# Routing's tiles, the order of loads, and two engine assignments in an attention and mixture-of-experts kernel

## The chip, the cores and the metric

The kernel runs on one core of one Trainium2 chip. The metric is the time on the device of one launch, in microseconds (us); lower is better. Before the change three runs gave 750.35, 750.99 and 751.72 us, a median of 750.99 us.

## What is computed

Three layers run one after the other. The first is bucketed attention over 8 heads of 768 tokens. The second is an expert layer with a top-1 choice and a capacity, the third an expert layer in which all eight experts see all tokens:

```python
x = attention(q, k, v, proj)                       # 768 x 512
logits = x @ w_gate                                # 768 x 8
expert_idx = argmax(logits, axis=1)
gate_w = softmax(logits)[expert_idx]
disp[e, pos] = x[i]                                # token i in the next free slot of its expert e
h = maximum(einsum('ecd,edf->ecf', disp, w1), 0)
y = einsum('ecf,efd->ecd', h, w2)
out[i] = gate_w[i] * y[expert_idx[i], pos[i]]      # the layer's output
P = sinkhorn(exp(out @ w_gate2))                   # 8 rounds of row and column scaling
out2 = sum over e of P[:, e] * (maximum(out @ w12[e], 0) @ w22[e])
```

## The kernel before

TensorE, ScalarE, VectorE and SyncE (DMA issue) execute their instructions in the order in which the program emits them. So the order of the Python calls is the order of each engine's queue.

**Attention** (to about 122 us) runs in an order from a list scheduler. Its tiles lie in pools at the left of on-chip memory and are given back when the function `attention` ends. At the right lie the first raw tiles of weights (`rawx`) behind a block `padx` of 112 words.

**The first expert layer** is `ffn` (L1286). Each expert has a tile of 128 slots. The weights come in 36 pieces of 1 MB (128 x 4 x 512 floats), in the fixed order of `stream`; nine raw tiles hold pieces on their way. `conv_next` (L351) takes the next piece and splits it in two halves: `split_w` (L330) emits for each half a copy by ScalarE that rounds to the high part (L337) and a subtraction that gives the low part (L339). The subtraction is VectorE's, but GpSimd's for both halves of the third piece (i == 2) and for a few later halves (`LO_POOL`). Then `conv_next` issues the load of the piece nine places on (L314, L316, or in four parts at L328). That load waits until the raw tile that it fills has been split.

`dispatch` (L1029) is routing. It is a generator: up to its first `yield`, some 25 short VectorE instructions (L1040 to L1088) find each token's slot, with two small matmuls (L1056, L1057) among 56 + 32 matmuls that only keep TensorE busy (L1055, L1059). Then six indirect DMAs from GpSimd's queue (L1092) scatter the tokens' rows to DRAM, to `xd`. The later parts are taken between the steps of the expert layer. Its small tiles come from a pool `tp` that is opened after attention's pools have been given back, in their place.

After routing, `ffn` issues three loads of slots' rows on SyncE's queue (`load_x`, L1173, from `xd`), splits four pieces (each with its load of a later piece on the same queue), and starts. For the low parts of the fourth piece the calls are kept in `los` and emitted inside the first `stage_a`. That `stage_a` does not read `xd`: it selects expert 0's tokens by a matmul with a one-hot matrix (L1194), copies the high part by ScalarE (L1180) and subtracts the low part by VectorE (L1181), in two halves. For the other experts `stage_a` transposes the loaded rows (L1187).

Then come the 36 steps, one piece of weights each: `g1` (L1201, product L1208, ReLU L1214), `tr` (L1216, transposes L1223, high part L1224, low part L1225) and `g2` (L1227, product L1234). A product takes 12 matmuls of 512 columns; for each of 4 blocks it uses high x high, high x low and low x high, so its second matmul already needs the low part of the weights, and its third the low part of the left factor. Acts such as a transposition are put in the middle of a step. At the end of an expert's second half of `g2`, its result is copied from PSUM to `ysb`, by VectorE (L1252) for experts 0 to 5 and by ScalarE (L1250) for expert 6. A DMA on ScalarE's queue writes it to `yd` (L1254), for experts 0 to 5 one step later. The PSUM tile of the result is one of two that `stage_a` uses as well.

**The second expert layer** (from about 262 us) keeps TensorE busy to 744 us.

Of the kernel before, what the change touches and what calls it, by code (L numbers as in the profile page):

```python
# [8 lines left out]
F32 = mybir.dt.float32  # L9
# [5 lines left out]
AF = mybir.ActivationFunctionType  # L15
# [6 lines left out]
P = 128  # L22
# [6 lines left out]
E = 8  # L29
# [18 lines left out]
POOL_END = 4 * 8 - 2 - NRAW - NRAWX  # L48
HI_DVE = ()
LO_POOL = (1,)  # L50
# [9 lines left out]
SQ = (33, 33)  # L60
CPAD = 0
SPAD = 160
OVR = 64
OVS = S - P
ZROW = E * P + NOV * OVR
# [158 lines left out]
def kernel(ctx: ExitStack, tc: tile.TileContext, consts, q, k, v, proj, wg, w1, w2, wg2, w12, w22, out, cap, dbg=None):  # L224
    nc = tc.nc
    f32 = lambda ap: ap.bitcast(F32)
    V = nc.vector
# [4 lines left out]
    cpool = ctx.enter_context(tc.tile_pool(name="cpool", bufs=1))  # L232
    rawp = ctx.enter_context(tc.tile_pool(name="rawp", bufs=NRAW))
    rawx = ExitStack()
    rawx.enter_context(tc.tile_pool(name="padx", bufs=1, side="right")).tile([P, 112], F32, name="padx")
    rawxp = rawx.enter_context(tc.tile_pool(name="rawx", bufs=NRAWX, side="right"))
    dpool = ctx.enter_context(tc.tile_pool(name="dpool", bufs=1, space=DRAM))

# [18 lines left out]
    seq = list(range(E - 1)) + [E, E - 1]  # L257
# [3 lines left out]
    for i in range(1, NV - 1):  # L261
        e, f = seq[i], seq[i + 1]
# [67 lines left out]
    def split_w(ts, raw, i, late=None):  # L330
        for z, t in enumerate(ts):
            sl = slice(2 * z, 2 * z + 2)
            n = (2 * i + z) % 8
            if 4 <= i < POOL_END and n in HI_DVE:
                V.tensor_copy(t[:, 0], raw[:, sl, :])
            else:
                nc.scalar.activation(out=t[:, 0], in_=raw[:, sl, :], func=AF.Copy)  # L337
            eng = nc.gpsimd if i == 2 or 4 < i < POOL_END and n in LO_POOL else V
            lo = lambda eng=eng, sl=sl, t=t: eng.tensor_tensor(  # L339
                out=t[:, 1], in0=raw[:, sl, :], in1=f32(t)[:, 0], op=ALU.subtract  # L340
            )
            if late is None:
                lo()
            else:
                late.append(lo)
# [5 lines left out]
    def conv_next(eng=nc.sync, late=None):  # L351
        i = cnt["conv"]
        if i >= len(stream) or i >= cnt["used"] + NHL:
            return False
        cnt["conv"] += 1
        raw = raw_t[i] if i == 4 * NV else raw_t.pop(i)
        ts = [hl_tile(2 * i + z) for z in range(2)]
        split_w(ts, raw, i, late)
        hl_t[i] = ts
        if cnt["load"] < cnt["limit"]:  # L360
            load_next(eng)
        return True
# [598 lines left out]
    def open_pool(st, name, bufs, **kw):  # L961
        return st.enter_context(tc.tile_pool(name=name, bufs=bufs, reuse_waits="tile", **kw))
# [63 lines left out]
        V.tensor_scalar(out=s, in0=inv, scalar1=-0.5, scalar2=200.0 * 2 ** 23, op0=ALU.mult, op1=ALU.add)  # L1026
        V.tensor_scalar(out=inv, in0=inv, scalar1=0.5, scalar2=54.0 * 2 ** 23, op0=ALU.mult, op1=ALU.add)

    def dispatch(tp, first, last):  # L1029
        t3 = lambda nm, dt=F32: tp.tile([P, NT, E], dt, name=nm)  # L1030
        te = lambda nm, dt=F32: tp.tile([P, E, NT], dt, name=nm)
        six = tp.tile([P, 8, NT], F32, name="six")
# [8 lines left out]
        cand = t3("cand")  # L1041
# [9 lines left out]
        ps = mm_tile()  # L1051
# [6 lines left out]
        for _ in range(NW[1]):  # L1058
# [3 lines left out]
            out=inc.rearrange("p e t -> p (e t)"), data0=col(C_MASK, E * NT), data1=oh.rearrange("p e t -> p (e t)"),  # L1062
# [16 lines left out]
            out=first, in0=col(C_S, P).unsqueeze(1).to_broadcast([P, NT, P]),  # L1079
# [11 lines left out]
        for t in range(NT):  # L1091
            i = nc.gpsimd.indirect_dma_start(  # L1092
                out=xd, out_offset=bass.IndirectOffsetOnAxis(ap=idxs[:, t:t + 1].bitcast(U32), axis=0),
                in_=x[:, t, :], in_offset=None,
# [8 lines left out]
        V.scalar_tensor_tensor(out=db, in0=jsc, scalar=float(OVR), in1=col(C_CE, E), op0=ALU.mult, op1=ALU.add)  # L1103
        V.tensor_single_scalar(out=keep, in_=pos1, scalar=float(cap), op=ALU.is_le)
        V.tensor_tensor(out=od, in0=oh, in1=xt(db), op=ALU.mult)
        ex = t3("ex")
        V.tensor_tensor(out=ex, in0=lg, in1=bt(mx), op=ALU.subtract)
        V.tensor_reduce(out=dbs, in_=od.rearrange("p e t -> p t e"), axis=AX.X, op=ALU.add)
        V.tensor_scalar_add(dbs, dbs, -float(OVR))
# [46 lines left out]
    def ffn_tools(st, bufs, xbufs):  # L1156
        p2 = open_pool(st, f"f{bufs}", bufs)
        dT, hs, hT, xe, yt = {}, {}, {}, {}, {}
        puts = []

        def onehot():
            t = p2.tile([P, 2, 512], F32, tag="hs", name="hs")
            return t.rearrange("p a n -> p (a n)")[:, 0:NT * P].rearrange("p (t n) -> p t n", n=P)
        W3 = ((0, 0), (0, 1), (1, 0))

        def load_x(e):
            t = p2.tile([P, DM], F32, tag="xe", name="xe", bufs=xbufs)
            r0 = e * P if e < E else E * P + (e - E) * OVS
            if e == E:
                for r in (0, OVR):  # L1170
                    nc.sync.dma_start(out=t[r:r + OVR], in_=xd[r0:r0 + OVR])
            else:
                nc.sync.dma_start(out=t, in_=xd[r0:r0 + P])  # L1173
            xe[e] = t

        def stage_a(e, oh0=None, late=None):
            d = dT[e] = p2.tile([P, 2, 512], F32R, tag="dT", name="dT")

            def split(sl, ps):
                nc.scalar.activation(out=d[:, 0, sl], in_=ps, func=AF.Copy)  # L1180
                V.tensor_tensor(out=d[:, 1, sl], in0=ps, in1=f32(d)[:, 0, sl], op=ALU.subtract)  # L1181

            if oh0 is None:
                t = xe.pop(e)
                ps = y_tile() if e <= E else mm_tile()
                for c in range(4):
                    nc.tensor.transpose(ps[:, c * P:(c + 1) * P], t[:, c * P:(c + 1) * P], ident)  # L1187
                split(slice(0, 512), ps)
                return
            for j in range(2):  # L1190
                ps = y_tile()
                for c in range(2):
                    for t in range(NT):
                        nc.tensor.matmul(  # L1194
                            ps[:, c * P:(c + 1) * P], lhsT=x[:, t, (2 * j + c) * P:(2 * j + c + 1) * P],
                            rhs=oh0[:, t, :], start=(t == 0), stop=(t == NT - 1),
                        )
                split(slice(j * 256, j * 256 + 256), ps[:, 0:256])
                late.pop(0)()

        def g1(e, half, w, mid=None):  # L1201
            if half == 0:
                hs[e] = p2.tile([P, 2, 512], F32, tag="hs", name="hs")
            ps = mm_tile()
            n = 0
            for c in range(4):
                for a, b in W3:
                    nc.tensor.matmul(  # L1208
                        ps, lhsT=dT[e][:, a, c * P:(c + 1) * P], rhs=w(b, c), start=(n == 0), stop=(n == 11)
                    )  # L1210
                    n += 1
                if mid and c == 1:
                    mid()
            nc.scalar.activation(out=hs[e][:, half, :], in_=ps, func=AF.Relu)  # L1214

        def tr(e, half):  # L1216
            if half == 0:
                hT[e] = p2.tile([P, 2, 2, 512], F32R, tag="hT", name="hT")
            h = hs[e] if half == 0 else hs.pop(e)
            ps = mm_tile()  # L1220
            for f in range(4):
                sl = slice(f * P, (f + 1) * P)
                nc.tensor.transpose(ps[:, sl], h[:, half, sl], ident)  # L1223
            nc.scalar.activation(out=hT[e][:, 0, half, :], in_=ps, func=AF.Copy)  # L1224
            V.tensor_tensor(out=hT[e][:, 1, half, :], in0=ps, in1=f32(hT[e])[:, 0, half, :], op=ALU.subtract)  # L1225

        def g2(e, half, w, mid=None):  # L1227
            if half == 0:
                yt[e] = psl.tile([P, 512], F32, tag="l", name="yl") if e >= E else y_tile()
            ps, t = yt[e], hT[e]  # L1230
            n = 12 * half
            for f in range(4):
                for a, b in W3:
                    nc.tensor.matmul(  # L1234
                        ps, lhsT=t[:, a, half, f * P:(f + 1) * P], rhs=w(b, f), start=(n == 0), stop=(n == 23)
                    )
                    n += 1
                if mid and f == 1:
                    mid()
            if half == 0:  # L1240
                return
            hT.pop(e)
            ps = yt.pop(e)
            if e == E:
                return ps
            if e == E - 1:
                return ps
            y = p2.tile([P, DM], F32, tag="ysb", name="ysb", bufs=1)
            if e == E - 2:
                nc.scalar.activation(out=y, in_=ps, func=AF.Copy)  # L1250
            else:
                V.tensor_copy(y, ps)  # L1252
            n, r0 = (P, e * P) if e < E else (OVR, E * P + (e - E) * OVR)
            put = lambda: nc.scalar.dma_start(out=yd[r0:r0 + n], in_=y[0:n])  # L1254
            if e < E - 2:
                puts.append(put)
            else:
                put()

        return onehot, puts, load_x, stage_a, g1, tr, g2  # L1260
# [25 lines left out]
    def ffn():  # L1286
        with ExitStack() as st:
            onehot, puts, load_x, stage_a, g1, tr, g2 = ffn_tools(st, 2, NXE)
            oh0 = onehot()
            ohs = {}  # L1290
            parts = dispatch(open_pool(st, "tp", 1), oh0, onehot)
            next(parts)
            for i in range(1, 4):
                load_x(seq[i])
            los = []
            for i in range(4):
                conv_next(late=los if i == 3 else None)
            done = 0

            def act(s):  # L1300
# [579 lines left out]
```

## Time and profile before

| | us |
|---|---|
| median of three runs | 750.99 |
| the profiled execution, its own time | 749.77 |
| its span, from first to last instruction | 748.0 |
| TensorE (PE) busy | 728.4 (97%) |
| VectorE (DVE) busy | 563.0 (75%) |
| ScalarE (ACT) busy | 467.5 (63%) |
| GpSimd (POOL) busy | 113.0 (15%) |

The granted clock is 1.000 for the whole span. A row of a timeline gives the start and the duration in us, the engine, the line of the kernel, the operation, what it writes and reads, and how many instructions are merged in it. In square brackets stands how long the engine was idle before, and what ended that. PE is TensorE's matmuls, SPq and ACTq the DMA issues of SyncE and ScalarE. Neighbouring matmuls overlap in a row, so the distance from start to start tells their pace.

### The profile page before, as it was taken

To read this page: it belongs to the slowest core of one execution; us is meant where nothing else is said; L and a number is where in the kernel's file an instruction comes from. 1 tells how busy PE (TensorE), PEld (TensorE's weight loads), DVE (VectorE), ACT (ScalarE), POOL (GpSimd) and SP (SyncE) were. 2 spreads that over 40 slices of the span, in tenths; PEclk is the share of its full clock that TensorE was granted. 3 is DMA by queue.
4 is the path that set the end of the run, shared out by engine and by line. 5 is a ranking of instruction groups with operands and counts; after the bars stand their busy time and mean duration, and the time that the engine had idled before them with its cause. 6 is when DMAs were issued, how large, how long until landed. Compare 5 with 4: busy or idle time off the path is not lost.

```text
span 748.0 us, 12294 instructions
## 1 busy us (share of the span) xinstructions
PE 728.4 (97%) x4770; PEld 467.4 (62%) x4770; DVE 563.0 (75%) x983; ACT 467.5 (63%) x761; POOL 113.0 (15%) x117
## 2 busy tenths in 40 slices
PE   8999998999999799999999999999999999999998
PEld 7889888777788556545546545545545545645654
DVE  5988997689998866887695785786785865866842
ACT  4799898488787678555653754664575375365420
POOL 5577863512100200000000000000000000000000
PEclk9999999999999999999999999999999999999999
DMA  9456549799997333422231131041032030000002
GB/s 238 104 142 180 152 142 383 266 376 376 385 389 292 87 113 113 169 77 94 61 110 55 49 121 57 4 164 59 1 114 112 1 113 1 1 0 1 1 1 84
DMA packets 61608, 97.02 MB, mean 130 GB/s; under 512 B 17603, under 2 KB 19059, under 8 KB 61546
## 3 DMA queue, kind: packets, MB, share of 16 engines
q1 hardware_dynamic: 53066, 82.21, 33.2%
q10 hardware_dynamic: 7520, 10.83, 4.1%
q0 software_dynamic: 960, 3.15, 1.3%
q8 instruction: 39, 0.64, 0.4%
q14 instruction: 23, 0.19, 0.1%
HBM read 79.99 MB, written 9.31 MB: 119 GB/s over the span
## 4 chain that ended last, share of the span: by engine, by line
PE 62%; DVE 2%; ACT 1%; issue 0%; DVEq 0%
PE b L1783 32%; PE b L1708 25%; PE b L1751 4%; DVE hl L1429 1%; DVE s L1616 1%; PE b L1546 1%; ACT junk L1009 0%; DVE q L1280 0%; DVE x L1799 0%; PE b L1505 0%; PE b L1017 0%; PE b L1493 0%; ACT hl L1426 0%; PE b L1593 0%; DVE x L1284 0%
## 5 line engine op out<-in xcount | busy, mean ns | idle before, releaser
L1783 PE MATMUL b<-hl,hT 128*128 128x512 f16 (+1 forms) x1176 | 252.0, 375 | 0.0
L1783 PEld LDWEIGHTS <-hT 128*128 128x128 f16 x1176 | 114.3, 98 | 129.1
L1708 PE MATMUL b<-xo,hl 128*128 128x384 f16 x1176 | 192.7, 326 | 0.0
L1708 PEld LDWEIGHTS <-hl 128*128 128x128 f16 x1176 | 114.8, 98 | 77.0 <-issue 0.8
L1429 DVE SCALAR_TENSOR_TENSOR hl<-raw,scl,hl 128x1024 f16<-128x1024 f32 x57 | 72.3, 1281 | 45.2 <-ACT hl L1426 45.2
L339 DVE TENSOR_TENSOR hl<-raw,hl 128x1024 fp32r<-128x1024 f32 x66 | 82.0, 1289 | 4.4 <-ACT hl L337 4.2
L1426 ACT ACTIVATE hl<-raw,scl 128x1024 f16<-128x1024 f32 x57 | 63.3, 1139 | 24.7 <-DVE scl L1020 24.7
L337 ACT ACTIVATE hl<-raw 128x1024 fp32r<-128x1024 f32 x72 | 71.8, 1062 | 0.4 <-ACT ysb L1250 0.4
L1009 ACT ACTIVATE junk<-raw 128x1024 bf16<-128x1024 f32 x64 | 67.2, 1050 | 1.0
L1801 DVE SCALAR_TENSOR_TENSOR x<-b,q,x 128x512 f32<-128x512 f32 (+1 forms) x43 | 31.5, 738 | 34.3 <-PE b L1783 34.0
L1208 PE MATMUL mm<-hl,dT 128*128 128x512 f32 x216 | 54.3, 398 | 1.6 <-DVE dT L1181 1.6
L763 POOL TENSOR_TENSOR plo<-pf,phi 128x768 f16<-128x768 f32 x30 | 49.7, 1666 | 24.6 <-ACT phi L759 12.2
L1681 DVE SCALAR_TENSOR_TENSOR hT<-tz,hT 128x384 f16<-128x384 f32 x44 | 24.1, 556 | 37.6 <-ACT hT L1680 37.5
L1680 ACT ACTIVATE hT<-tc 128x384 f16<-128x384 f32 x28 | 14.7, 525 | 60.1 <-DVE tc L1677 60.1
L1234 PE MATMUL y<-hl,hT 128*128 128x512 f32 x192 | 50.0, 402 | 2.2 <-POOL hl L339 1.1
L698 DVE TENSOR_REDUCE mz<-mm 128x1 f32<-128x384 f32 x96 | 47.6, 550 | 2.9 <-PE mm L691 2.6
L1426 ACT ACTIVATE hl<-s,scl 128x1024 f16<-128x1024 f32 x28 | 31.5, 1148 | 28.4 <-DVE s L1616 21.5
L752 ACT ACTIVATE pf<-mm 128x384 f32<-128x384 f32 x96 | 41.8, 488 | 8.4 <-PE mm L745 6.6
L1208 PEld LDWEIGHTS mm<-hl,dT 128*128 128x128 f32 x216 | 39.4, 188 | 10.6 <-DVE dT L1181 2.4
L745 PE MATMUL mm<-q,k 128*128 128x384 f32 x192 | 45.1, 353 | 0.0
L1234 PEld LDWEIGHTS y<-hl,hT 128*128 128x128 f32 x192 | 34.6, 188 | 11.2 <-POOL hl L339 1.9
L759 ACT ACTIVATE phi<-pf 128x768 f16<-128x768 f32 x46 | 38.7, 848 | 1.2
(280 smaller groups left out, 1003.9 us busy)
## 6 DMA issues: line engine op xcount, KB each, us to landing
raw<-in_moe_w_dram SPq DMA_DIRECT2D x48, 1024.0 KB, 8.3
raw<-in_moe_w_dram SPq DMA_DIRECT2D x48, 256.0 KB, 5.5
raw<-in_moe_w_dram ACTq DMA_DIRECT2D x8, 1024.0 KB, 5.0
xd<-zer SPq DMA_DIRECT2D x13, 256.0 KB, 3.1
xe<-xd SPq DMA_DIRECT2D x7, 256.0 KB
yd<-ysb ACTq DMA_DIRECT2D x7, 256.0 KB, 4.5
qkin<-in_q_dram SPq DMA_DIRECT2D x8, 192.0 KB, 4.6
vin<-in_v_dram SPq DMA_DIRECT2D x4, 384.0 KB
```

The costliest lines, as they stand in the source:

```text
L337: nc.scalar.activation(out=t[:, 0], in_=raw[:, sl, :], func=AF.Copy)
L339: lo = lambda eng=eng, sl=sl, t=t: eng.tensor_tensor(out=t[:, 1], in0=raw[:, sl, :], in1=f32(t)[:, 0], op=ALU.subtract)
L698: V.tensor_reduce(out=mz[h][:, a, t:t + 1], in_=b.ps[:, 0:HW], axis=AX.X, op=ALU.max)
L745: nc.tensor.matmul(ps[:, 0:HW], lhsT=kk[h][:, tok(t)], rhs=qq[h][:, half(a)], start=(i == 0), stop=(i == 1))
L763: eng.tensor_tensor(out=lo[h, t], in0=pf[h, t], in1=hi[h, t], op=ALU.subtract)
L1009: nc.scalar.activation(out=junk[:, 0:n], in_=src, func=AF.Square, accum_out=acc)
L1208: nc.tensor.matmul(ps, lhsT=dT[e][:, a, c * P:(c + 1) * P], rhs=w(b, c), start=(n == 0), stop=(n == 11))
L1234: nc.tensor.matmul(ps, lhsT=t[:, a, half, f * P:(f + 1) * P], rhs=w(b, f), start=(n == 0), stop=(n == 23))
L1426: nc.scalar.activation(out=slot[n][:, 0], in_=src() if src else total[n], func=AF.Copy, scale=sw)
L1429: V.scalar_tensor_tensor(out=slot[n][:, 1], in0=src() if src else total.pop(n), scalar=sw, in1=slot[n][:, 0], op0=ALU.mult, op1=ALU.subtract,)
L1708: nc.tensor.matmul(ps, lhsT=w[:, a, c, j * P:(j + 1) * P], rhs=xo[:, o, b, c, :], start=(n == 0 and not again), stop=(n == 5), skip_group_ ...
L1783: nc.tensor.matmul(ps, lhsT=hT[:, a, 2 * r + f, t * P:(t + 1) * P], rhs=w[:, b, f, cs], start=(r == 0 and n == 0), stop=(r == 3 and n == 5),)
```

## The change

Four edits. Routing's pool `tp` is opened at the start, at the right of memory, in a place of its own; `padx` shrinks from 112 to 40 words, and the tile `ex` uses `cand`'s place. The loads of slots' rows come after the first two calls of `conv_next` (one) and after all four (two), and no longer before them. The third piece's low parts go to VectorE. The results of experts 0 to 5 are copied from PSUM by ScalarE.

```diff
@@ tile_attn_moe_kernel @@
-    rawx.enter_context(tc.tile_pool(name="padx", bufs=1, side="right")).tile([P, 112], F32, name="padx")
+    rawx.enter_context(tc.tile_pool(name="padx", bufs=1, side="right")).tile([P, PADX], F32, name="padx")
+    tp = rawx.enter_context(tc.tile_pool(name="tp", bufs=1, side="right"))
@@ split_w @@
-            eng = nc.gpsimd if i == 2 or 4 < i < POOL_END and n in LO_POOL else V
+            eng = nc.gpsimd if 4 < i < POOL_END and n in LO_POOL else V
@@ dispatch @@
-    def dispatch(tp, first, last):
+    def dispatch(first, last):
...
-        ex = t3("ex")
+        ex = cand
@@ ffn_tools, g2 @@
             y = p2.tile([P, DM], F32, tag="ysb", name="ysb", bufs=1)
-            if e == E - 2:
-                nc.scalar.activation(out=y, in_=ps, func=AF.Copy)
-            else:
-                V.tensor_copy(y, ps)
+            nc.scalar.activation(out=y, in_=ps, func=AF.Copy)
@@ ffn @@
-            parts = dispatch(open_pool(st, "tp", 1), oh0, onehot)
+            parts = dispatch(oh0, onehot)
             next(parts)
-            for i in range(1, 4):
-                load_x(seq[i])
             los = []
             for i in range(4):
                 conv_next(late=los if i == 3 else None)
+                if i == 1:
+                    load_x(seq[1])
+            for i in range(2, 4):
+                load_x(seq[i])
```

## Rows read from the trace of the kernel before

**Rows 1.** TensorE's waits, 120 to 260 us: total, times, longest.
```profile
PE mm L1208 <- DVE dT L1181: 1.6, 2, 1.0
PE y L1234 <- DVE ysb L1252: 1.0, 2, 0.8
```

**Rows 2.** Timeline of DVE, end of attention to the first product.
```profile
122.10 0.21 DVE L793 TENSOR_TENSOR lg<-lg,lt 128x48 f32<-128x48 f32 x1
124.54 0.20 DVE L1040 TENSOR_REDUCE six<-lg 128x6 f32<-128x48 f32 x1 [2.23 <-POOL sv L986]
...
126.23 0.17 DVE L1068 TENSOR_SCALAR ov<-mm 128x8 f32<-128x8 f32 x1
...
128.85 0.17 DVE L1088 TENSOR_TENSOR idxs<-six 128x6 int32<-128x6 f32 x1
128.96 4.63 DVE L339 TENSOR_TENSOR hl<-raw,hl 128x1024 fp32r<-128x1024 f32 x4
133.50 0.42 DVE L1181 TENSOR_TENSOR dT<-y,dT 128x256 fp32r<-128x256 f32 x1
...
134.97 0.42 DVE L1181 TENSOR_TENSOR dT<-y,dT 128x256 fp32r<-128x256 f32 x1
```

**Rows 3.** Timeline of POOL, the same stretch and on.
```profile
123.50 1.01 POOL L814 TENSOR_TENSOR x<-num,eu 128x384 f32<-128x384 f32 x1 [1.49 <-ACT num L809]
...
129.89 1.38 POOL L1092 DMA_INDIRECT xd<-x,idxs  x1 [5.33 <-issue]
...
137.66 0.96 POOL L1092 DMA_INDIRECT xd<-x,idxs  x1 [0.30 <-issue]
138.65 4.72 POOL L339 TENSOR_TENSOR hl<-raw,hl 128x1024 fp32r<-128x1024 f32 x2
```

**Rows 4.** Timeline of PE, from the filling matmuls to expert 1's transposes.
```profile
120.99 3.29 PE L1055 MATMUL mm<-tri,ones 128*128 128x128 f16 x56
126.00 0.17 PE L1056 MATMUL mm<-s,tri 128*128 128x8 f16 x1 [1.72 <-DVE s L1050]
...
133.72 4.41 PE L1208 MATMUL mm<-hl,dT 128*128 128x512 f32 x18
...
139.79 0.40 PE L1234 MATMUL y<-hl,hT 128*128 128x512 f32 x1
141.08 1.42 PE L1234 MATMUL y<-hl,hT 128*128 128x512 f32 x5 [0.89 <-POOL hl L339]
...
142.70 0.48 PE L1234 MATMUL y<-hl,hT 128*128 128x512 f32 x1
143.42 2.79 PE L1234 MATMUL y<-hl,hT 128*128 128x512 f32 x11 [0.24 <-POOL hl L339]
146.05 0.60 PE L1187 MATMUL y<-ident,xe 128*128 128x128 f32 x4
```

**Rows 5.** Timeline of DVE and of POOL in a later part of routing.
```profile
174.08 0.90 DVE L1124 TENSOR_SCALAR six<-six 128x6 f32<-128x6 f32 x1
...
172.44 2.50 POOL L339 TENSOR_TENSOR hl<-raw,hl 128x1024 fp32r<-128x1024 f32 x1 [10.66 <-ACT hl L337]
```

**Rows 6.** The copies to ysb: instructions, shortest/median/longest ns, first and last start.
```profile
L1252 DVE COPY ysb<-y x6: 675/682/692, 148.1 to 225.6; 128x512 f32<-128x512 f32 x6
L1250 ACT ACTIVATE ysb<-y x1: 601/601/601, 237.1 to 237.1; 128x512 f32<-128x512 f32 x1
```

**Rows 7.** Timeline of ACT, a wait for the first product of a later expert.
```profile
212.89 0.60 ACT L1214 ACTIVATE hs<-mm 128x512 f32<-128x512 f32 x1 [1.36 <-PE mm L1208]
```

**Rows 8.** Timeline of SP's DMA issues, 118 to 149 us.
```profile
120.24 9.27 SPq L328 DMA_DIRECT2D raw<-in_moe_w_dram  x14
...
140.39 1.27 SPq L1173 DMA_DIRECT2D xe<-xd  x3
141.76 6.98 SPq L328 DMA_DIRECT2D raw<-in_moe_w_dram  x12
```

**Rows 9.** Line 1092, the six scatters: issue to landing.
```profile
DMA to landing us min/median/max: 2.7/3.6/6.4
```

More of the change, by code (lines that the diff above doesn't have):

```diff
@@ L62 @@
 SPAD = 160
+PADX = 40
 OVR = 64
```

## The prediction
> **What bounds the kernel now.** The table of busy times comes first: TensorE is busy for 97% of the span, at the full clock, so an edit on another engine gains only where TensorE waits for that engine. TensorE's waits come second, cut to the stretch that the diff touches, 120 to 260 us. Two kinds in it belong to the change: products held by the copy to `ysb` and products held by the low parts of `dT` [rows 1]. The timelines of VectorE, GpSimd and TensorE around routing come third. The reader should see a relay: attention's last addition to `lg` starts at 122.10 and takes 0.21, then VectorE is idle for 2.23 us until GpSimd is through with attention's tiles [rows 2, 3]; TensorE runs its filling matmuls and then is idle for the count [rows 4]; later it is idle twice for GpSimd's low parts of the third piece, which GpSimd can only begin at 138.65, behind the six scatters [rows 3, 4]. The issues of SyncE come last: it stands from about 129.5 to 140.39 at the first load of slots' rows, and weights go on behind it [rows 8]. From 262 us on nothing in the diff acts; TensorE runs through there, so that what the first expert layer gains or loses should reach the end undiminished.
>
> **Routing's tiles.** The wait for GpSimd goes, since the tiles no longer lie where attention's did. At most the 2.2 us of idle time is gained [rows 2]. What is late next is TensorE's own queue: the count (L1056) stands behind 56 filling matmuls, whose row ends at 124.28 [rows 4], so it can start near 124.1 and no longer at 126.00. L1068 follows it by 0.23 us, as now; it moves from 126.23 to about 124.35, a gain of 1.9. A second thing may be late. L1124, a VectorE instruction on 6 columns, took 0.90 us and ended at 174.98, when GpSimd's subtraction had just ended (174.94) [rows 5]; its neighbours of that size take 0.17 [rows 2]. Routing's short instructions would now run beside GpSimd's L814, from 123.50 to 124.51 [rows 3]. Held to its end, L1068 starts near 124.7: a gain of 1.5. I take 1.5, since L1124 is the nearest row to that case, and keep 1.3 and 1.9 as ends.
> The Trainium skill (SBUF — State Buffer, section "SBUF: two separate sides") says that VectorE and GpSimd share one pair of ports, and that the first to take it holds it for its whole instruction. By that rule the term is the 1.5, without it the 1.9; the 0.90 us agrees with it.
>
> **The third piece's low parts.** VectorE's queue gets two subtractions between the second piece's and the first split of `stage_a`. Four take 4.63, so two take 2.3 [rows 2]. Against the 1.5 gained, both splits (L1181) come 0.8 later; the second ends at 136.2 and no longer at 135.39. In TensorE's queue the ninth matmul of the first product needs it. Matmuls follow one another by 0.24 (eleven in 2.79, the last of 0.40), so the ninth stands at 133.72 + 8 x 0.24 = 135.64, 0.25 after the split [rows 2, 4]. It will start 0.6 later. Behind it wait the ReLU, the transposes and `g2`: a loss of 0.6, with ends 0.2 (if routing gains 1.9) and 0.8.
> In return both of TensorE's waits on GpSimd go. By starts: 141.08 - 139.79 - 0.24 = 1.05 and 143.42 - 142.70 - 0.24 = 0.48 [rows 4], together 1.5. The low parts are there by 134.5, before their products. So the first three edits' part in this place is 1.5 - 0.6 = **0.9 gained**, from 0.7 to 1.3.
>
> **The order of the loads.** Eight quarter loads of weights move ahead of the rows. At 0.58 each (twelve in 6.98) they take 4.7 us of SyncE, from 129.5 to about 134.2, in the time in which it now stands still [rows 8]. Each waits for its raw tile: the first piece's is split by about 129.8, the second's by 132.2, so the first load of rows is at its wait before the scatters have landed. Rows for the next two experts then stand behind four more quarter loads and one whole load, some 2.9 us; they are due one and two experts later. Weights come 12 us earlier, worth nothing: no wait of TensorE or ScalarE in this stretch ends with a load of weights. I take zero; the other end is the slower rival.
>
> **The copies of results.** VectorE loses six copies of 0.68, ScalarE gets six of 0.60 [rows 6]. VectorE ran the one for expert 2 far behind its product, and TensorE was idle for 0.8 on it [rows 1]; by starts, as an idle of 0.89 was 1.05 above [rows 4], about 1.0. ScalarE will reach that copy as soon as it has done the transposes' high part, several us before the PSUM tile is wanted: **1.0 gained**. The other, shorter wait of this kind (0.2) comes ahead of the longest wait for a split (1.0) [rows 1], which takes it up: nothing. On ScalarE the copy must wait for the last matmuls of `g2`, and two roundings of weights queue behind it, 1.5 to 2 us late. Cover: ScalarE stands idle for 1.36 at the next ReLU [rows 7], and the pieces are split ahead of their use. Without that cover it would cost up to 0.5 for each of six experts. The relief of VectorE by 4.1 us of work I count at zero: ahead of the long wait for a split it was held to the end of GpSimd's subtraction anyway [rows 5]. The other end is that it also ends the 1.6 us of these waits [rows 1].
>
> **Sum.** 0.9 + 1.0 = 1.9 us. The profiled execution took 749.77 us itself, with 748.0 us of span; it should take 747.9. It lies 1.2 us under the median of the runs, 750.99, and I carry the difference over: **749.1 us**.
>
> **Rivals.** *The splits are freed as well.* VectorE, without the copies, catches up, routing gains the full 1.9, and the 1.6 us of waits for the splits go too: 1.9 + 0.4 + 1.6 = 3.9, 747.1 us. For it speaks VectorE's backlog behind those waits; against it L1124, which shows a VectorE that waits for GpSimd, not for room. Chance 0.14.
> *The waits only move.* Either routing is bound elsewhere (the wait of 2.23 was for something besides the tiles, so that the edit doesn't do what it says), and the low parts then cost 2.1 and return 1.5, or ScalarE's copies hold the weights and take back what the one wait gave. Then 0.4 remains, 750.6 us. For it: six copies in a queue that must wait for TensorE; against it: ScalarE's idle time. Chance 0.22.
> *The rows come late*, the slower one. The scatters run beside the subtractions and now beside 2 MB of weights that were not in flight. Expert 1's transposes are due at 146.05 - 0.9 = 145.1 [rows 4]. The scatters start at about 128.4 and, at the pace of the first row, 1.38 + 0.30 [rows 3], the last is issued at 136.8. A landing takes 2.7 to 6.4 [rows 9]; with 0.4 for the issue of the load and the same bounds for its own landing, the rows arrive between 142.6 and 150.0. At the late end TensorE waits 4.9 and the kernel is 3.0 slower, 754.0 us; it decides for slower by over 0.2% from an arrival at 148.5 on. For it: the first scatter, issued while weights were in flight, has the 6.4. Against it: GpSimd issues a scatter only every 1.55 us on average, (137.66 - 129.89) / 5 [rows 3]. Chance 0.09.
> The same section of the Trainium skill has a rule that would bring this about: VectorE's two-port operations keep GpSimd from writing the descriptors of the DMAs that it issues. Here the first scatter, beside the subtractions, took 1.38 and the last, with VectorE idle, 0.96 [rows 3]: a hint of it, not the several-fold stretch that the page reports.
>
> **How the numbers follow.** The forecast has 0.55, the rivals 0.14, 0.22 and 0.09. A measurement of this kernel can tell about 0.2%, 1.5 us, from no change. The forecast's own ends are 0.7 + 0.8 = 1.5 and 1.3 + 1.0 + a little, 2.5, so nine tenths of it is faster; with the first rival about 0.62. Same has the rest of it and the moved waits, 0.29; slower 0.09. The range runs from the first rival, 747.1, to somewhat over the moved waits and the mild cases of late rows, 751.4.
>
> **What would show it.** In the changed profile: L1040 right behind L793 without idle time, L1068 within 124.3 to 124.9; the second L1181 ending near 136.2; GpSimd's L339 four times, not six, and no wait of L1234 on it; L1187 first at about 145.1 with no idle time ahead of it; no wait on `ysb`; the stretch from 262 us on the same but 1.9 earlier. The prediction is wrong if L1187 waits for rows, if roundings behind ScalarE's copies hold products, or if the gain is seen at 250 us and lost by the end.

## The result, and the profile after

The changed kernel is slower: a median of 755.84 us over 12 runs (752.72 to 761.88) beside 751.34 us (749.32 to 753.89) for the kernel before in the same session, a ratio of 1.0053 with a 95% interval of 1.0031 to 1.0076. The profiled execution took 752.84 us itself, with a span of 751.1 us, 3.1 us more than before; its mean granted clock is 0.997. Lines of the changed kernel are 1 to 2 higher than those of [rows 1 to 9] (L1183 is the old L1181, L1210 the old L1208).

TensorE's waits of the changed kernel, 120 to 260 us (total, times, longest), beside [rows 1]:
```profile
PE mm L1210 <- DVE dT L1183: 2.8, 2, 1.8
PE y L1189 <- DMA xe<-xd: 2.7, 2, 1.8
PE mm L1210 <- DVE hT L1227: 2.5, 1, 2.5
PE b L1494 <- DVEq L1392: 1.3, 1, 1.3
PE mm L1225 <- ACT hs L1216: 0.7, 1, 0.7
```
The waits on `ysb` and on GpSimd's low parts are gone, as forecast. In their place stand a wait for slots' rows (2.7), one for the low part of a transposed block (2.5, none before) and one for a ReLU of ScalarE (0.7). These three make 5.9 us. The wait for the low parts of `dT` has grown from 1.6 to 2.8.

Routing on VectorE, then the end of its last split, beside [rows 2]; then GpSimd, beside [rows 3]:
```profile
121.51 0.21 DVE L795 TENSOR_TENSOR lg<-lg,lt 128x48 f32<-128x48 f32 x1
121.75 0.20 DVE L1042 TENSOR_REDUCE six<-lg 128x6 f32<-128x48 f32 x1
...
123.07 0.96 DVE L1063 TENSOR_TENSOR_SCAN inc<-cst,oh 128x48 f32<-128x48 f32 x1
...
124.01 0.15 DVE L1070 TENSOR_SCALAR ov<-mm 128x8 f32<-128x8 f32 x1
...
126.72 6.90 DVE L341 TENSOR_TENSOR hl<-raw,hl 128x1024 fp32r<-128x1024 f32 x6
133.54 0.42 DVE L1183 TENSOR_TENSOR dT<-y,dT 128x256 fp32r<-128x256 f32 x1
...
135.00 0.42 DVE L1183 TENSOR_TENSOR dT<-y,dT 128x256 fp32r<-128x256 f32 x1
```
```profile
122.89 1.02 POOL L816 TENSOR_TENSOR x<-num,eu 128x384 f32<-128x384 f32 x1 [1.48 <-ACT num L811]
...
136.23 1.17 POOL L1094 DMA_INDIRECT xd<-x,idxs  x1 [0.30 <-issue]
```
L1042 follows attention's last addition without idle time. The scan L1063 is held until GpSimd's L816 ends (122.89 + 1.02 = 123.91, and the next instruction starts at 123.95). In the kernel before it runs after that subtraction and takes 0.25:
```profile
125.87 0.25 DVE L1061 TENSOR_TENSOR_SCAN inc<-cst,oh 128x48 f32<-128x48 f32 x1
```
From L795 to L1070 it is 2.50 us, where [rows 2] have 126.23 - 122.10 = 4.13.

TensorE from the first product to expert 2's transposes, beside [rows 4]:
```profile
131.48 0.71 PE L1210 MATMUL mm<-hl,dT 128*128 128x512 f32 x2
134.01 4.04 PE L1210 MATMUL mm<-hl,dT 128*128 128x512 f32 x16 [1.82 <-DVE dT L1183]
...
139.72 1.53 PE L1236 MATMUL y<-hl,hT 128*128 128x512 f32 x6
...
141.44 3.02 PE L1236 MATMUL y<-hl,hT 128*128 128x512 f32 x12
146.22 0.63 PE L1189 MATMUL y<-ident,xe 128*128 128x128 f32 x4 [1.76 <-DMA xe<-xd]
...
153.48 0.63 PE L1189 MATMUL y<-ident,xe 128*128 128x128 f32 x4 [0.92 <-DMA xe<-xd]
```
`g2` runs without a gap (six and twelve matmuls, where [rows 4] have three interruptions). But the transposes stand idle for expert 1's rows and again for expert 2's. SyncE's first load of rows and the landing of the scatters, beside [rows 8, 9]:
```profile
142.75 0.33 SPq L1175 DMA_DIRECT2D xe<-xd  x1
143.17 1.80 SPq L330 DMA_DIRECT2D raw<-in_moe_w_dram  x4
145.08 0.38 SPq L318 DMA_DIRECT2D raw<-in_moe_w_dram  x1
145.56 2.15 SPq L1175 DMA_DIRECT2D xe<-xd  x4
```
```profile
DMA to landing us min/median/max: 6.2/6.4/6.5
```
The last scatter is issued 1.43 us earlier than before (136.23, not 137.66), yet the load that waits for it comes 2.36 later. Every scatter takes 6.2 us or more to land; before it was 2.7 at best and 3.6 in the median. Expert 2's rows are issued behind five more loads of weights. The stretch in which the scatters land (from the right: GB/s, the share of the DMA engines, the clock):
```profile
136.00:138.00 2.00, 2.00 (x10) 1.56 (x10) 0.56 (x1) 0.60 (x1) 1.17 (x1) 1.00 1.04 405
```
The same two us of the kernel before have 164 GB/s and a share of 0.42:
```profile
136.00:138.00 2.00, 2.00 (x11) 1.56 (x10) 0.52 (x1) 0.60 (x1) 1.50 (x2) 1.00 0.42 164
```

The place of the new wait for a low part, on TensorE, VectorE and GpSimd; then the granted clock (third column from the right) of the stretches around it:
```profile
184.63 2.55 PE L1210 MATMUL mm<-hl,dT 128*128 128x512 f32 x10 [0.97 <-DVE dT L1183]
189.72 2.30 PE L1210 MATMUL mm<-hl,dT 128*128 128x512 f32 x6 [2.54 <-DVE hT L1227]
...
184.50 4.57 DVE L341 TENSOR_TENSOR hl<-raw,hl 128x1024 fp32r<-128x1024 f32 x2
188.99 0.68 DVE L1227 TENSOR_TENSOR hT<-mm,hT 128x512 fp32r<-128x512 f32 x1
...
184.45 2.40 POOL L341 TENSOR_TENSOR hl<-raw,hl 128x1024 fp32r<-128x1024 f32 x1 [7.98 <-ACT hl L339]
```
```profile
185.00:190.00 5.00, 2.46 (x11) 1.76 (x10) 5.00 (x4) 5.00 (x8) 1.85 (x1) 1.00 0.91 333
190.00:195.00 5.00, 5.00 (x18) 3.99 (x18) 4.90 (x7) 1.13 (x3) 0.00 (x0) 0.66 0.92 268
```
The next product does not read `hT`; what it needs is a bank of PSUM that L1227 has not yet read (e6 tries this reading). VectorE comes to it late, because its subtractions run beside one on GpSimd (the first of the two at 184.50 is held, 4.57 for both and not 2.4). In the kernel before the two take 4.08 in this place, and no product waits for `hT`. Behind the idle time the clock is granted at 0.66 over five us, between its two levels, 1.2 and 2.4 GHz, and six matmuls take 2.30 where 1.64 is usual (the same form at 138.25).

### The profile page after: what moved, and what is told of

Read it like the earlier page. It is cut to its first block, busy times and chain, and to the rows that moved or that the text cites. A ratio compares the mean times of both kernels' runs of the same rounds, so it can differ in the third digit from the quotient of the medians.

```text
span 751.1 us, 12289 instructions
## 1 busy us (share of the span) xinstructions
PE 728.5 (97%) x4770; PEld 468.2 (62%) x4770; DVE 563.8 (75%) x979; ACT 470.5 (63%) x767; POOL 110.4 (15%) x115
## 3 DMA queue, kind: packets, MB, share of 16 engines
q0 software_dynamic: 960, 3.15, 1.3%
## 4 chain that ended last, share of the span: by engine, by line
PE 84%; DVE 5%; DMA 4%; issue 3%; ACT 2%; POOL 1%; SPq 0%; ACTq 0%; DVEq 0%; POOLq 0%
PE b L1784 31%; PE b L1709 25%; PE mm L747 4%; PE b L1752 4%; PE av L774 4%; PE mm L1210 4%; PE y L1236 4%; PE mm L693 2%; DVE hl L341 1%; PE mm L667 1%; DMA xe<-xd 1%; POOL xd L1094 1%; DMA xd<-x,idxs 1%; DMA vin<-in_v_dram 1%; PE yl L1236 1%
## 5 line engine op out<-in xcount | busy, mean ns | idle before, releaser
L341 DVE TENSOR_TENSOR hl<-raw,hl 128x1024 fp32r<-128x1024 f32 x68 | 84.8, 1289 | 8.4 <-ACT hl L339 8.2
L1210 PE MATMUL mm<-hl,dT 128*128 128x512 f32 x216 | 55.8, 406 | 5.3 <-DVE dT L1183 2.8
L1210 PEld LDWEIGHTS mm<-hl,dT 128*128 128x128 f32 x216 | 40.0, 192 | 15.0 <-DVE dT L1183 3.7
```

The lines of the kernel that those rows point to most:

```text
L341: lo = lambda eng=eng, sl=sl, t=t: eng.tensor_tensor(out=t[:, 1], in0=raw[:, sl, :], in1=f32(t)[:, 0], op=ALU.subtract)
L1210: nc.tensor.matmul(ps, lhsT=dT[e][:, a, c * P:(c + 1) * P], rhs=w(b, c), start=(n == 0), stop=(n == 11))
```

## The experiments

All ratios are to the kernel before on the same chip. The changed kernel and e1 to e10 have twelve runs each, e11 six and e12 five. **Tiles**, **order**, **low parts** and **copies** are the four edits.

To see where each kernel gains or loses, I take from each trace the start of the transposes of the first, second, third, fifth and seventh set of slots' rows, and of the next layer's first matmuls (transposes); from each I subtract the start of attention's last addition to `lg`, and then the same difference of the kernel before. (After, first set: 146.22 - 121.51 = 24.71; before: 146.05 - 122.10 = 23.95 [rows 2, 4]; +0.76.) The last column compares the time from there to the end of the span. Plus is later.

| kernel | ratio | 1st | 2nd | 3rd | 5th | 7th | next layer | rest |
|---|---|---|---|---|---|---|---|---|
| after | 1.0053 | +0.76 | +2.09 | +1.30 | +5.17 | +4.67 | +3.41 | +0.28 |
| e1 order | 1.0047 | +0.26 | +2.25 | +1.46 | +2.26 | +2.24 | +1.84 | -0.05 |
| e2 all but order | 1.0008 | -1.15 | -0.92 | -1.18 | +1.52 | +0.11 | +0.12 | +1.49 |
| e3 all but copies | 1.0037 | +0.35 | +1.83 | +1.02 | +1.86 | +1.82 | +2.29 | +0.01 |
| e4 tiles, low parts | 1.0002 | +0.27 | +0.27 | +0.25 | +0.25 | +0.22 | +0.19 | -0.07 |
| e5 copies | 1.0033 | -0.02 | +0.20 | -0.03 | +3.87 | +2.70 | +1.44 | +1.91 |
| e6 copies, old banks | 1.0012 | -0.03 | +0.19 | -0.04 | +0.67 | -0.80 | -0.06 | -0.02 |
| e7 split first | 0.9993 | -3.40 | -3.40 | -3.30 | -2.71 | -2.73 | -0.13 | +0.02 |
| e8 e7 and e6 | 1.0019 | -3.37 | -3.15 | -3.04 | -1.97 | -3.45 | -0.18 | -0.02 |
| e9 e7, own result | 0.9966 | -3.36 | -3.36 | -3.37 | -2.99 | -3.02 | -3.90 | -0.02 |
| e10 own result | 0.9998 | -0.02 | -0.02 | -0.02 | -0.03 | -0.04 | -1.30 | +1.68 |
| e11 e8, own result | 0.9937 | -3.38 | -3.17 | -3.21 | -2.14 | -3.61 | -3.93 | +1.33 |
| e12 one load ahead | 1.0082 | -0.04 | +4.53 | +5.31 | +5.81 | +5.77 | +5.47 | +1.66 |

A row is one execution, a ratio the middle of many; a fall of the clock can stand in the one and not in the other.

### The edits apart: e1 to e5

e1 is the kernel before with the order of the loads alone:
```diff
-            for i in range(1, 4):
-                load_x(seq[i])
             los = []
             for i in range(4):
                 conv_next(late=los if i == 3 else None)
+                if i == 1:
+                    load_x(seq[1])
+            for i in range(2, 4):
+                load_x(seq[i])
```


> The kernel before with one edit: the new order of the loads (two loads of weights ahead of the slots' rows). Theory A, rows late: the weights fill the DMA engines while the scatters run, the last scatter lands 5 us or more after its issue and not 2.7, expert 1's transposes wait 1.5 us or more for their rows, and the kernel is 2 to 4 us slower than before. Theory B, PSUM banks: the loss in the changed kernel comes from the copies on ScalarE, so this one is within 1 us of before. Theory C, clock: the loss is TensorE's clock, which falls because of the gap that the earlier routing leaves ahead of the first product; granted clock 1.000 here and no loss.

Measured: 754.33 us, ratio 1.0047 (1.0028 to 1.0066). Expert 1's transposes, at which the expectation looked, are only 0.26 late; expert 2's wait 1.8 us for rows, and 1.8 is still there where the next layer begins:
```profile
154.74 0.63 PE L1188 MATMUL y<-ident,xe 128*128 128x128 f32 x4 [1.80 <-DMA xe<-xd]
```
The order by itself costs about as much as the whole change. Its profiled execution shows 1.8 us of the 3.5 us (0.47%) by which the runs differ; where the rest falls is open.

e2 is the change without that edit (the three loads of rows stand ahead of the splits again).

> The changed kernel with the old order of the loads. Theory A: no transpose waits for rows, the gain of the other three edits is seen, 1 to 3 us faster than before. Theory B: the wait of 2.5 us for the transposed block's low part ahead of expert 4's second half stays, with a fall of the clock behind it; 1 to 4 us slower than before. Theory C: granted clock below 1.000 with the loss in the gap at 131 to 134 us; 3 us or more slower than before.

Measured: 751.59 us, ratio 1.0008 (0.9987 to 1.0028). So the order costs the changed kernel 1.0053 - 1.0008, 0.45% or 3.4 us. The other three edits lead by 1.15 us at expert 1, as forecast, and then lose 2.7 us between the third and the fifth set. The wait of 2.5 stands there again, with the clock at 1.00 behind it.

e3 is the change without the copies on ScalarE (`V.tensor_copy(y, ps)` for experts 0 to 5 again), e4 the same without the order as well.

> The changed kernel with the copies of results on VectorE again; the PSUM tiles then lie in the banks of before. Theory A: rows still late by about 1.8 and 1.3 us; 1 to 3 us slower than before. Theory B: the wait ahead of expert 4's second half is gone and the old wait of 0.8 us for the copy is back; within 1 us of before. Theory C: as in the changed kernel, 3 us or more slower, granted clock below 1.000.

> The kernel before with two edits: routing's tiles in their own pool and the third piece's low parts on VectorE. Theories A and B: what the prediction said of these two, about 1.0 us faster than before, the gap of some 2 us ahead of the third matmul of the first product included, granted clock 1.000. Theory C: the gap lowers the clock, granted clock below 1.000 and 2 us or more slower.

Measured: e3 753.8 us, ratio 1.0037 (1.0017 to 1.0057); e4 751.49 us, ratio 1.0002 (0.9979 to 1.0025). Neither has the wait of 2.5 for L1227: it belongs to the copies. And e4, the two edits that I was surest of, gains nothing. Its trace shows why. TensorE's first product in e4, then the clock of that stretch:
```profile
132.44 0.72 PE L1210 MATMUL mm<-hl,dT 128*128 128x512 f32 x2
134.97 5.51 PE L1210 MATMUL mm<-hl,dT 128*128 128x512 f32 x16 [1.81 <-DVE dT L1183]
```
```profile
135.00:140.00 5.00, 5.00 (x15) 3.94 (x16) 2.51 (x3) 0.60 (x1) 2.74 (x3) 0.66 0.54 210
```
Routing is earlier, so TensorE starts its first product earlier, but VectorE has six subtractions to do ahead of the first split: TensorE now stands idle for 1.81 in mid-product, and behind it the clock falls to 0.66. Sixteen matmuls take 5.51 where the changed kernel, with the same idle time and the clock at 1.00, takes 4.04: 1.5 us, more than the 1.15 by which the same edits lead in e2, where the clock stays at 1.00.

e5 is the copies alone:
```diff
-            if e == E - 2:
-                nc.scalar.activation(out=y, in_=ps, func=AF.Copy)
-            else:
-                V.tensor_copy(y, ps)
+            nc.scalar.activation(out=y, in_=ps, func=AF.Copy)
```


> The kernel before with one edit: the results of experts 0 to 5 are copied by ScalarE. Theory B (banks): the products' tiles lie in other PSUM banks than before; the first product of expert 4's second half waits about 2.5 us for the low part of expert 3's transposed block (the line of the low part of hT), the waits for the copy are gone; 1 to 2 us slower than before. Rival B2 (queue): the copies only hold ScalarE's queue; no such wait, 0.5 to 1 us of waits for ReLUs or roundings, within 1 us of before.

Measured: 753.37 us, ratio 1.0033 (1.0014 to 1.0052). The edit that was to gain 1.0 loses 3.9 us between the third and the fifth set, with the wait of 2.5 and a clock of 0.91 and 0.75 from 185 to 195 us.

### What the edits bring with them: e6 to e8

The products' PSUM tiles rotate over five banks in a sequence that the framework works out when the kernel is built. In the built programs the sequence is the same as before in every kernel here that leaves the copies alone, and another one in the changed kernel, e2 and e5. The first tile that differs is that of expert 4's second product: with the copies on ScalarE it gets the bank of expert 3's first transposed block, which L1227 reads, and in the kernel before that of an earlier tile. e6 is e5 with the old sequence written down by hand (`MM_BANKS`, 63 numbers, not shown):
```diff
+    mm_bank = iter(MM_BANKS)
...
-    psm = open_pool(ps2, "psm2", 5, space=PSUM)
+    psm = open_pool(ps2, "psm2", 1, space=PSUM)
...
-        return psm.tile([P, 512], F32, tag="mm", name="mm")
+        return psm.tile([P, 512], F32, tag=f"mm{next(mm_bank)}", name="mm")
```


> The run before this one, with the tiles of the products and transposes put in the same sequence of PSUM banks as in the kernel before. Theory B: the wait of 2.5 us is gone, and so are the waits for the copy; 1.5 to 3 us faster than the copies alone, 0.5 to 1 us faster than before. Rival B2: the banks don't matter, the same as the copies alone within 0.5 us.

Measured: 751.11 us, ratio 1.0012 (0.998 to 1.0044). The same place of TensorE in e6:
```profile
182.96 2.81 PE L1211 MATMUL mm<-hl,dT 128*128 128x512 f32 x11 [0.98 <-DVE dT L1184]
186.31 1.43 PE L1211 MATMUL mm<-hl,dT 128*128 128x512 f32 x5 [0.55 <-DVE hl L341]
```
The wait of 2.54 is gone with the banks. The intervals of e5 and e6 overlap, so this rests on the traces: the wait stands in the three profiles with the new sequence (after, e2, e5) and in none of the three that have the copies and the old one (e6, e8, e11). The copies' own effect can now be read in the table: from the third set to the fifth they lose 0.7 (the 0.55 above, and 0.47 for a ReLU of ScalarE), from the fifth to the seventh they gain 1.5, where the waits on `ysb` were.

e7 is e4 with the low parts of the third piece, like those of the fourth, behind the first split:
```diff
-                conv_next(late=los if i == 3 else None)
+                conv_next(late=los if i >= 2 else None)
...
             stage_a(0, oh0, los)
+            for lo in los:
+                lo()
```


> The run of tiles and low parts, with the third piece's low parts moved behind the first split of expert 0's rows on VectorE. Theory C (clock, as now stated: the gap of about 2 us ahead of the first product's third matmul costs its own length and makes the clock fall in part of the executions): the gap is closed to under 0.5 us, the granted clocks are again those of the kernel before (mean loss about 0.3%), 3 to 4.5 us faster than before. Rival C2 (the clock falls for another reason): the span loses the gap, but granted clocks stay as in the run of tiles and low parts (mean loss about 0.5%), 1.5 to 2.5 us faster than before.

Measured: 750.22 us, ratio 0.9993 (0.9975 to 1.0011). TensorE's first product, then ScalarE's copy of expert 6's result and TensorE's first wait behind it, in e7:
```profile
132.68 4.37 PE L1210 MATMUL mm<-hl,dT 128*128 128x512 f32 x18
```
```profile
226.94 0.52 ACTq L1256 DMA_DIRECT2D yd<-ysb  x1
...
237.60 0.60 ACT L1252 ACTIVATE ysb<-y 128x512 f32<-128x512 f32 x1 [4.20 <-SPq L1395]
...
241.16 0.66 PE L1225 MATMUL mm<-ident,hs 128*128 128x128 f32 x4 [1.69 <-ACT hs L1216]
```
The first product runs through. Over the twelve runs the mean granted clock is 0.998 here (0.998 in the kernel before beside it) and 0.995 in e4 (0.997), so what was expected of the clock came true, and the gain in time did not. In the trace TensorE leads by 3.4 us at expert 1 and by 2.7 at the seventh set. At the next layer only 0.1 is left. The copy at 237.60 needs the one tile `ysb`, and that comes free when the write of expert 5's result, issued at 226.94 behind 1 MB loads for the next layer on the same queue, has landed. The landing does not move with TensorE: the kernel before, with its write issued at 229.04, has this copy at 237.1 [rows 6], behind 1.64 us of idle time:
```profile
237.09 0.60 ACT L1250 ACTIVATE ysb<-y 128x512 f32<-128x512 f32 x1 [1.64 <-SPq L1391]
```
Counted from attention's last addition to `lg`, it stands at 114.8 to 115.2 us in the kernel before, e2, e4, e6, e7 and e8, although the write is issued at 102.3 to 107.2. ScalarE's roundings and ReLUs stand behind it. (The releaser that the row names, SPq L1395, writes no `ysb`; the wait is for several, and this reading of it is what e9 tries.)

e8 is e7 with the copies and the old banks.

> The split-first run with the copies on ScalarE and the old sequence of banks. Theories B and C: the two gains add up, 4 to 5.5 us faster than before. Rivals B2 and C2: no faster than the split-first run, or slower than it by 1 us or more.

Measured: 752.75 us, ratio 1.0019 (0.9998 to 1.0039). It leads by 3.45 us at the seventh set and loses 3.3 by the next layer, in the same place.

### The hidden bound, and the version without it: e9 to e11

In e9 expert 6's result goes to a free tile of the slots' rows; e10 is the kernel before with that alone, e11 is e8 with it.
```diff
-            y = p2.tile([P, DM], F32, tag="ysb", name="ysb", bufs=1)
+            own = e == E - 2
+            y = p2.tile([P, DM], F32, tag="xe" if own else "ysb", name="ysb", bufs=xbufs if own else 1)
```


> The kernel of e7 (routing's tiles in their own pool; the low parts of the third and fourth pieces on VectorE, behind the first split), and expert 6's result goes to a free tile of the slots' rows instead of the one tile ysb. Theory (the write of expert 5's result, whose landing sets free ysb, took back what e7 had gained): ScalarE's copy of expert 6's result no longer has the 4.2 us of idle time on its own queue ahead of it, the waits of 1.69 and 0.69 on TensorE behind it go, and the 2.1 us by which e7 led at 208 us reach the end: about 2.4 us under e7, 747.8 us beside a before of 751, ratio 0.996. Rival (the next layer's start is bound by something else, such as the gather of the results behind the same writes): the wait at 241 us goes and comes back as a wait at 255 to 265 us; 750.2 us, ratio 0.999.

> The kernel before with that one edit alone: expert 6's result goes to a free tile of the slots' rows. There ScalarE's copy of it had 1.64 us of idle time ahead of it. Theory (the landing takes back only what is gained ahead of it): TensorE arrives later in this kernel, so little stands behind the copy: 0 to 0.7 us gained, 750.4 to 751.1 us beside a before of 751. Rival (the single tile costs the kernel before as much as e7): 2 us gained, 749 us.

> As e9, with the results copied by ScalarE as in the change and the products in the PSUM banks that they have in the kernel before: three of the change's four edits, each with what its side effect costs taken away. Theory (the copies by themselves gain the waits on ysb, 1.0 us, once the landing no longer takes it back): 1.0 us under e9, about 746.8 us beside a before of 751. Rival (ScalarE has no time for the copies: the products then wait for its roundings and ReLUs, as e6 hinted with three short waits for 1.7 us): as e9 or up to 1 us over it, 747.8 to 748.8 us.

Measured: e9 748.01 us, ratio 0.9966 (0.9949 to 0.9983); e10 750.88 us, 0.9998 (0.9977 to 1.0018); e11 747.12 us, 0.9937 (0.9917 to 0.9957), each beside 750.69 us. The same copy in e9:
```profile
232.84 0.60 ACT L1253 ACTIVATE ysb<-y 128x512 f32<-128x512 f32 x1
```
It stands at 232.84 with no idle time ahead of it, 4.5 us earlier than in e7 (counted from attention's last addition), and the lead reaches the next layer (-3.90) and the end. In the kernel before the same edit gives 1.3 us up to the next layer, in one execution, and nothing that the medians can tell; an effect of that size is within their interval, so whether the landing costs the kernel before anything stays open. What is won ahead of the landing it does take back: e7 and e9 differ by this tile alone, and by 2.2 us in their medians (their intervals overlap a little; the traces show where it is won).

e11 beats both kernels. It has three of the change's four edits, with the third piece's low parts behind the first split and the two mends of e6 and e9. Whether the copies themselves add anything to e9 is not settled: the two intervals overlap, and the table has them level at the next layer (-3.93 and -3.90).

### How the order costs: e12

e12 is e1 with `i == 0` for `i == 1`: expert 1's rows behind one piece's load.

> The kernel before with the order of the loads alone, but the first load of slots' rows stands behind one piece's load (1 MB) and no longer behind two. Theory (the rows come late because the loads of weights that were put ahead of them are under way when the scatters write their rows): half the weights, so the scatters land earlier by about 1 MB at 400 GB/s, 2.6 us: expert 1's transposes wait under 0.5 us and not 1.8 us; expert 2's may still wait, since its rows stand behind the other three loads as in e1. Some 1 to 1.8 us under e1: 752.5 to 753.3 us beside a before of 751. Rival (it is not the weights in flight but the landing of the scatters itself, late for any order): 754.3 us, as e1. Second rival (one load ahead is hidden entirely): 751.

Measured: 757.97 us, ratio 1.0082 (1.0059 to 1.0104), worse than e1, which none of the three had (the two intervals just overlap; the table has +5.47 beside +1.84 at the next layer). TensorE's two sets of transposes, then SyncE's issues, in e12:
```profile
145.28 0.60 PE L1188 MATMUL y<-ident,xe 128*128 128x128 f32 x4
155.78 0.63 PE L1188 MATMUL y<-ident,xe 128*128 128x128 f32 x4 [4.41 <-DMA xe<-xd]
```
```profile
141.43 0.33 SPq L1174 DMA_DIRECT2D xe<-xd  x1
141.86 3.90 SPq L329 DMA_DIRECT2D raw<-in_moe_w_dram  x8
145.86 0.38 SPq L317 DMA_DIRECT2D raw<-in_moe_w_dram  x1
146.34 4.23 SPq L1174 DMA_DIRECT2D xe<-xd  x4
```
The theory holds for expert 1: its rows are loaded at 141.43, 2.65 us earlier than in e1 (144.08), and nothing waits for them. It left out that the other pieces' loads then go between the first rows and the second. Expert 2's rows stand behind 3 MB (eight quarters and a whole load), behind 2 MB in e1 and behind none in the kernel before; they land 9.7 us after their issue, 7.9 in e1, and TensorE waits 4.41, 1.80 and 0 for them. The wait grows with that dose, so the cause is the weights ahead of the second rows, and not only those ahead of the first.

## Why the prediction was wrong

**Routing's tiles**: right. 1.5 gained was forecast, with L1070 2.6 behind L795; it is 2.50, a gain of 1.63, and what comes next is the lock that the prediction read from L1124: a scan that takes 0.25 us in the kernel before lasts 0.96 and ends with GpSimd's L816 (0.95 or 0.96 in every profile with this edit). The Trainium skill (SBUF — State Buffer, section "SBUF: two separate sides") has the two engines share a pair of ports that the first one holds for its whole instruction; this trace agrees.

**The third piece's low parts**: right in the sum, incomplete in what follows. Up to the wait for rows TensorE is 1.00 us earlier (0.76 - 1.76), where 0.9 was forecast; e2 has 1.15. Both waits on GpSimd are gone. What the step did not count is the idle time that it opens. I priced the second split and the ninth matmul; the first split is late as well, and TensorE stops for 1.8 us behind two matmuls. In two of the four profiles with this gap (e3, e4; not in the changed kernel and e2) the clock falls behind it, worth 1.5 us. With the same low parts behind the first split (e7) the same two edits lead by 3.4, not 1.0: a small part of the gain was in where routing's work went, the larger part in what stood ahead of the split.

**The order of the loads** is the step that failed first: "I take zero". The working counted SyncE's time to issue the loads, 4.7 us ahead of the first rows and "some 2.9 us" ahead of the next, and never the time of the 2 MB that each of these groups moves; at the 405 GB/s of the stretch shown above, 2 MB is 5 us. The rows of experts 1 and 2 come 1.76 and 0.92 late, and e1 and e2 put the edit at 0.45 to 0.47%, 3.4 to 3.5 us. The rival "the rows come late" had half of the mechanism, scatters that land late beside the weights, at a chance of 0.09. It watched expert 1 only, with its rows deciding from 148.5 us on; they came at 146.2. Of the two readings of it, GpSimd held up in writing descriptors and transfers that compete, the runs speak for the second: the last scatter of the changed kernel is issued earlier than before, and what grew is the time from issue to landing. In e1 GpSimd issues its six scatters at the pace of the kernel before, beside the same work of VectorE, and they land after 5.9 to 7.1 us.

**The copies of results**: the 1.0 is there, the cost is not "cover". In e6, e8 and e11, between the fifth set of transposes and the sixth (not in the table), TensorE gains 1.08 us on the kernel before, in each: this is the forecast's term. Ahead of it 0.7 to 1.1 go for ScalarE's lateness, in the one place without cover; the forecast had named "up to 0.5 for each of six experts" without cover, and counted nothing. Over both lies a cost that no reading of the trace of before could show: a new sequence of PSUM banks, a wait of 2.54 and the clock behind it, 3.9 us in e5.

**That gains reach the end "undiminished"**: wrong. The copy of expert 6's result waits for a landing near 237 us that does not move; e7 lost 2.6 us to it. The row was in the trace of before ([rows 6], and 1.64 us of idle time ahead of it), and I had read it as a duration only. The changed kernel itself is 4.67 late at the seventh set and 3.41 at the next layer, where it waits 1.26 and the kernel before 2.28. That the same bound hides this part of the loss is not shown: e1 and e12, 2.24 and 5.77 late, get back only 0.4 and 0.3.

So of 3.1 us in the profiled execution, attention gave -0.6 by chance; tiles and low parts -1.0; late rows +2.3 net of what later waits took up; the banks, the clock behind them and the late ReLU +3.9; -1.8 came back by the end of the layer, and the next layer has +0.3.

## What to carry to other kernels

When a load is moved ahead of another, price the bytes at the rate of that stretch, for every later load of the queue, and not the issues; the first reader may be on time and the second late. Ask of each gain where the next thing stands that does not move with it (here a write's landing into a single tile), because there it is taken back, and a good edit looks worthless until that is mended. After any edit of who reads a PSUM tile, compare the bank of each later tile: the wait of 2.5 us came from there and not from the work that was moved.

## What had not been expected of the hardware

The granted clock fell after waits of TensorE in the middle of dense work: 0.66 over 135 to 140 us behind an idle time of 1.8 us (e3, e4), 0.66 over 190 to 195 us behind 0.97 and 2.54 (after); yet it stayed at 1.00 behind the same 1.8 us in the changed kernel and in e2, and in e2 behind the wait of 2.5 as well. An idle time so costs itself and, some of the time, more: 1.5 us behind the 1.8 (e4 beside the changed kernel), 1.2 us behind the 2.5 (after beside e2, third to fifth set). Five of the fourteen profiles (e2, e5, e10, e11, e12) have 1.3 to 1.9 us more from the next layer's start to the end, each with a clock below 1.00 somewhere from 255 to 270 us; in e1, e4 and e7 such a fall, at 255 us, costs nothing by this count. This alone makes one execution of a kernel differ from the next by more than some of the effects studied here.

The indirect writes take longer to land beside loads of weights, although they go by a queue of their own: 2.7 us at best and 3.6 in the median in the kernel before, 4.5 and 6.1 with 1 MB put ahead of the first rows (e12), 6.2 and 6.4 (after) or 5.9 and 6.6 (e1) with 2 MB.
